# Wider reads in the K, V and FFN weight loads of a decode block

## The chip, the cores and the metric

The kernel runs on one core of a Trainium2 chip. The metric is the device time of one execution in microseconds (us). It was measured three times; the median is what is compared. A profile of one further execution, taken by the hardware profiler, is read for the causes. In it PE is TensorE's matmuls, PEld its weight loads, DVE is VectorE, ACT ScalarE, POOL GpSimd, and SP (SPq) the queue of SyncE, which here only issues DMAs.

## The reference

One token for each of four batches goes through a layer norm; its output feeds attention over the last 4096 positions of a K/V cache and, in parallel, a gated feed-forward block. Both results are added to the input. All tensors are bfloat16.

```python
B, Sq, D = 4, 1, 512;  Hq, Hkv, Sk, Dh = 32, 8, 16384, 128;  F = 1792;  W = 4096
xn = layernorm(x)
q = (xn @ wq)                                     # 32 heads of 128
k, v = k_cache[:, :, Sk - W:, :], v_cache[:, :, Sk - W:, :]   # each of 8 kv heads serves 4 q heads
p = softmax(q k^T * Dh**-0.5)
A = (p v) @ wo
Bf = (silu(xn @ w_gate) * (xn @ w_up)) @ w_down
out = x + A + Bf
```

The K and V windows are 33.6 MB each, the weights about 14 MB together: the kernel reads 81.01 MB from HBM for four rows of output.

## The kernel before

The attention is cut into 16 steps (`ND`). Step d takes kv head d // 2 for two of the four batches (the first two where d is even, the last two where it is odd). Its K is 2 x 4096 rows of 128 values, 2 MB, and is loaded by one DMA as a tile of 128 partitions by 16 KB: a partition holds 64 (`NT`) consecutive positions of one batch. Function `kv_ap` (L167) gives the order of partitions: position group first, batch second, so partition 2q belongs to the first batch and 2q + 1 to the second. V is loaded by the same pattern. K and V each have two buffers (`KB`, `VB`), taken in turn.

For each step TensorE transposes K in 64 pieces of 128 x 128 (L386), VectorE copies the transposes from PSUM to SBUF (L300), and TensorE computes scores for the 8 heads of both batches against every partition. Since a partition belongs to one batch, the scores of the other batch's heads are pushed to minus 1e30 by a small matmul (`mask`, L377) that multiplies `mkr`, a 2 x 128 table of which partition is whose, by `mkc`. GpSimd builds `mkr` at the start (L190, L205). Then come the row maximum (L305), the shift (L405), the exponential (L271), the denominators and the product with V (`pv`, L409). The first half of a step's V product runs while the next step's scores run.

SyncE issues all the large loads on one queue, in this order: W_q (`WQ`); K of steps 0 and 1; W_gate and W_up (`WG`, `WU`); V of step 0; then K of step d and V of step d - 1 for d = 2 to 15; W_down (`WD`); V of step 15 in two halves of each partition's row (`load_v_half`, L232); and W_o (`WO`) in five pieces cut by `WO_CUTS`. K of step d waits until step d - 2's transposes are finished (`s_tr`), V of step d until the product of the step before is finished (`s_pv`, the counter starts with one). WG, WU and WD hold rows of 14 KB in each of 128 partitions, `WQ` rows of 32 KB. The two halves of the last V have semaphores of their own (`d_v[1]` and `d_vz`), so that TensorE can begin with the first half (L461) and waits for the second at L462.

After the 16 steps TensorE multiplies W_gate and W_up (L452), the last V, W_down, and then the 32 rows of W_o (`out_rows`, L171), each piece behind its semaphore. `spin` (L424) issues matmuls whose results nobody reads. Two copies and one 4 KB DMA write the output.

Of the kernel before, what the change touches and what calls it, by code (L numbers as in the profile page):

```python
# [2 lines left out]

# [2 lines left out]
ALU = mybir.AluOpType  # L6
# [4 lines left out]
def bass_parallel_sum__sliding_block_cached__swiglu_ffn__decode_kernel(  # L11
# [13 lines left out]
    _, HKV, Sk, Dh = A_k_cache.shape  # L25
    HQ = A_wq.shape[1] // Dh
    F = B_w_gate.shape[1]
    W = min(4096, max(256, Sk // 4))
# [6 lines left out]
    ND = B * HKV // 2  # L35
    C = 2 * REP
    NT = 2 * W // 128
    HT = NT // 2
    NG = 4
    KVN = NT * Dh  # L40
    HKN = HT * Dh
    SN = NT * C
# [11 lines left out]
    WG = sb("wg_sb", [128, NC, F], BF16)  # L54
    WU = sb("wu_sb", [128, NC, F], BF16)
    WD = sb("wd_sb", [128, NF, D], BF16)
    WO = sb("wo_sb", [128, NO, D], BF16)
    KB = sb("kbuf", [128, 2 * KVN], BF16)
    VB = sb("vbuf", [128, 2 * KVN], BF16)
# [6 lines left out]
    mkr = sb("mkr", [2, 128], BF16)  # L66
# [49 lines left out]
    d_wg = sem("d_wg")  # L116
    d_wu = sem("d_wu")
    d_wd = sem("d_wd")
# [3 lines left out]
    d_k = [sem("d_k%d" % s) for s in range(2)]  # L122
    d_v = [sem("d_v%d" % s) for s in range(2)]
    d_vz = sem("d_vz")
# [36 lines left out]
    wg_ap = B_w_gate.rearrange("(p c) n -> p c n", c=NC)  # L161
    wu_ap = B_w_up.rearrange("(p c) n -> p c n", c=NC)
    wd_ap = B_w_down.rearrange("(p t) n -> p t n", t=NF)
    wo_ap = A_wo.rearrange("(p c) n -> p c n", c=NO)
    ds = bass.ds

    def kv_ap(cache, d):  # L167
        b0 = d % 2 * 2
        return cache[b0:b0 + 2, d // 2, Sk - W:, :].rearrange("b (q t) d -> q b (t d)", t=NT)

    def out_rows(eng, c0, c1):  # L171
        for c in range(c0, c1):
# [7 lines left out]
    with nc.Block() as block:  # L180

        @block.gpsimd
        def _(eng):
            eng.memset(ident[:], 0.0)
            eng.memset(I4[:], 0.0)
            eng.memset(I8[:], 0.0)
            eng.memset(I4w[:], 0.0)
            eng.memset(rep[:], 0.0)
            eng.memset(ones[:], 1.0)
            eng.memset(mkr[:], -BIG)  # L190
            eng.memset(mkc[:], 1.0)
            eng.drain()
            eng.affine_select(I4[:], I4[:], pattern=[[-1, B]], compare_op=ALU.not_equal,
                              fill=1.0, base=0, channel_multiplier=1)
            eng.affine_select(ident[:], ident[:], pattern=[[-1, 128]], compare_op=ALU.not_equal,
                              fill=1.0, base=0, channel_multiplier=1)
            eng.affine_select(I8[:], I8[:], pattern=[[-1, C]], compare_op=ALU.not_equal,
                              fill=1.0, base=0, channel_multiplier=1)
            eng.affine_select(I4w[:], I4w[:], pattern=[[-1, 64]], compare_op=ALU.not_equal,
                              fill=1.0, base=0, channel_multiplier=1)  # L200

            eng.affine_select(rep[:], rep[:], pattern=[[1, REP], [-1, 128]], compare_op=ALU.not_equal,
                              fill=1.0, base=0, channel_multiplier=REP)

            eng.affine_select(mkr[:], mkr[:].rearrange("j (q b) -> j q b", b=2),  # L205
                              pattern=[[0, 64], [-1, 2]], compare_op=ALU.not_equal,
                              fill=0.0, base=0, channel_multiplier=1)
            eng.affine_select(mkc[:], mkc[:].rearrange("j (b h) -> j b h", b=2),
                              pattern=[[-1, 2], [0, REP]], compare_op=ALU.is_equal,
                              fill=0.0, base=0, channel_multiplier=1)  # L210
            eng.memset(XnT[:].bitcast(FP32), 0.0)
            eng.memset(QZ[:].bitcast(FP32), 0.0)
            eng.drain()
            eng.engine_nop().then_inc(s_const, 1)
            eng.memset(P[:], 1.0)
            eng.memset(VB[:, HKN:].bitcast(FP32), 0.0)  # L216
            eng.drain()
            eng.engine_nop().then_inc(s_const, 1)
            eng.engine_nop().then_inc(d_v[1], 16)

        @block.sync
        def _(eng):
            def load_k(d):
                if d >= 2:
                    eng.wait_ge(s_tr, 2 * NG * (d - 1))
                eng.dma_start(KB[:, d % 2 * KVN:(d % 2 + 1) * KVN], kv_ap(A_k_cache, d)).then_inc(d_k[d % 2], 16)

            def load_v(d):
                eng.wait_ge(s_pv, d + 1)
                eng.dma_start(VB[:, d % 2 * KVN:(d % 2 + 1) * KVN], kv_ap(A_v_cache, d)).then_inc(d_v[d % 2], 16)  # L230

            def load_v_half(d, h, done):  # L232
                a = d % 2 * KVN + h * HKN
                eng.dma_start(VB[:, a:a + HKN], kv_ap(A_v_cache, d)[:, :, h * HKN:(h + 1) * HKN]).then_inc(done, 16)

            def load_wo(n):
                a, b = WO_CUTS[n], WO_CUTS[n + 1]
                eng.dma_start(WO[:, a:b, :], wo_ap[:, a:b, :]).then_inc(d_wo[n], 16)

            eng.dma_start(WQ[:], wq_ap).then_inc(d_wq, 16)  # L240

            eng.wait_ge(s_xc, 1)
            load_k(0)
            load_k(1)
            eng.dma_start(WG[:], wg_ap).then_inc(d_wg, 16)
            eng.dma_start(WU[:], wu_ap).then_inc(d_wu, 16)
            load_v(0)
            for d in range(2, ND):
                load_k(d)
                load_v(d - 1)  # L250
            eng.dma_start(WD[:], wd_ap).then_inc(d_wd, 16)
            eng.wait_ge(s_pv, ND)
            load_v_half(ND - 1, 0, d_v[1])
            load_v_half(ND - 1, 1, d_vz)
            for n in range(len(d_wo)):
                load_wo(n)
# [19 lines left out]
        def _(eng):  # L276
# [17 lines left out]
            last.then_inc(s_qz, 1)  # L294
            eng.engine_nop().then_inc(s_ev, NG)

# [59 lines left out]
        def _(eng):  # L356
# [52 lines left out]
            def pv(bank, s, n):  # L409
                p = bank * PS  # L410
                if s == 0:
                    eng.wait_ge(d_v[bank], n[0])
                    eng.wait_ge(s_p, n[1])
                    eng.wait_ge(s_nrm, n[1])
                    for j in range(SN // 128):
                        mm(den_ps, ones[:], P[:, p + 128 * j:p + 128 * (j + 1)], start=(j == 0))
                for t in range(HT):
                    a = bank * KVN + s * HKN + 128 * t
                    o = p + C * (s * HT + t)
                    last = mm(O_wide, VB[:, a:a + 128], P[:, o:o + WIDE], start=(s == 0 and t == 0))  # L420
                if s == 1:
                    last.then_inc(s_pv, 1)
# [11 lines left out]
            with eng.Fori(0, ND // 2) as r:  # L434
                for b in range(2):
                    n = 2 * r + (b + 1)
                    ev = 4 * NG * r + 2 * NG * b
                    q = lambda w, b=b: QF[:, ds(r * (2 * WIDE) + b * WIDE, w)]
# [19 lines left out]
                last.then_inc(done, 1)  # L458
            for n in range(2):
                mm(ps_acc[64 * n:64 * n + 64, 0:256], I4w[:], X[:, 256 * n:256 * n + 256], start=True)  # L460
            pv(1, 0, (8 * ND + 16, ND + 1))  # L461
            eng.wait_ge(d_vz, 16)  # L462
            pv(1, 1, None)
            eng.wait_ge(s_guT, 1)
            eng.wait_ge(d_wd, 16)
# [58 lines left out]
```

## Time and profile before

| What | Value |
|---|---|
| Time, median of 3 | 195.99 us (195.85, 195.99, 196.53) |
| The profiled execution's own time | 195.84 us |
| Its span, first to last instruction | 194.6 us |
| Granted TensorE clock | 1.000 |
| PE busy, DVE busy | 161.6 us, 114.7 us |
| Read from HBM | 81.01 MB, 416 GB/s over the span |

The span is what the trace shows; 1.24 us of the profiled execution's time lie outside it. The DMA lines of a page count packets. SP's queue is called q1 there: it carried 6048 packets. 42 DMAs of 128 rows are 5376 rows, and each DMA ends with one 4-byte write on each of 16 DMA engines, which makes 672 more: 6048. So at present each row of a destination partition is one packet. The share of a queue is the sum of its packets' recorded durations over 16 engines' time; as the records of neighbouring packets overlap a little, it can pass 100%.

### The profile page before, as it was taken

How to read it: one execution, taken by the hardware profiler on the slowest of the kernel's cores; microseconds unless marked ns; L12 is line 12 of the kernel's file. 1: busy time of each engine (PE TensorE's matmuls, PEld its weight loads, DVE VectorE, ACT ScalarE, POOL GpSimd, SP SyncE). 2: the span in 40 equal slices, each digit the busy share in tenths (PEclk: the TensorE clock that was granted, in tenths of full speed). 3: DMA queues.
4: the chain of work that ended last, by engine and by line, in shares of the span. 5: the costliest groups of instructions: out<-in, count | busy, mean ns of one | idle time of the engine just before them, and what ended most of it. 6: DMA issues, size and time to landing. Idle time of an engine off the chain costs nothing. (4 is left out here: it accounts for less than half of the span.)

```text
span 194.6 us, 7758 instructions
## 1 busy us (share of the span) xinstructions
PE 161.6 (83%) x3466; PEld 138.9 (71%) x3466; DVE 114.7 (59%) x250; ACT 17.0 (9%) x27; POOL 10.3 (5%) x23
## 2 busy tenths in 40 slices
PE   0127997549898989898989898989898989898995
PEld 0113895548888878787878787878787878787752
DVE  1004775527676767676767676767676767675620
ACT  5700101001010101010101010101010101010100
POOL 8930000000000000000000000000000000000000
DMA  6999999999999999999999999999999999999992
GB/s 216 431 428 431 440 428 419 433 424 431 431 431 431 431 431 431 431 431 431 431 431 431 434 431 431 431 431 431 431 431 431 431 431 431 431 429 421 436 412 111
DMA packets 6070, 81.10 MB, mean 417 GB/s; under 512 B 680, under 2 KB 816, under 8 KB 1072
## 3 DMA queue, kind: packets, MB, share of 16 engines
q1 hardware_dynamic: 6048, 81.01, 97.7%
q8 instruction: 5, 0.08, 0.1%
q10 hardware_dynamic: 16, 0.01, 0.0%
q14 instruction: 1, 0.01, 0.0%
HBM read 81.01 MB, written 0.00 MB: 416 GB/s over the span
## 5 line engine op out<-in xcount | busy, mean ns | idle before, releaser
L300 DVE COPY kT<-ps_kt 128x1024 bf16<-128x1024 bf16 x128 | 79.4, 683 | 27.7 <-PE ps_kt L386 27.7
L386 PE MATMUL ps_kt<-ident,kbuf 128*128 128x128 bf16 x1024 | 62.8, 219 | 12.9 <-DMA kbuf<-in_A_k_cache_dram 11.9
L386 PEld LDWEIGHTS ps_kt<-ident,kbuf 128*128 128x128 bf16 x1024 | 57.3, 98 | 18.2 <-issue 18.2
L358 PE MATMUL ps_o<-p,vbuf 128*128 128x64 bf16 x1120 | 38.4, 193 | 0.0
L358 PEld LDWEIGHTS ps_s<-qz,kT 128*128 128x128 bf16 x1024 | 31.4, 98 | 6.6 <-issue 3.6
L358 PEld LDWEIGHTS ps_o<-p,vbuf 128*128 128x128 bf16 x1120 | 35.2, 98 | 1.1
L358 PE MATMUL ps_s<-qz,kT 128*128 x1024 | 34.7, 192 | 1.2
L271 ACT ACTIVATE p<-ps_s 128x512 bf16<-128x512 f32 x17 | 10.1, 597 | 162.1 <-PE ps_s L358 162.1
L305 DVE TENSOR_REDUCE rm<-ps_s 128x8 bf16<-128x512 f32 x17 | 11.7, 691 | 21.2 <-PE ps_s L358 21.2
L358 PE MATMUL ps_o<-p,ones 128*128 128x128 bf16 (+1 forms) x69 | 6.9, 220 | 3.3 <-DMA vbuf<-in_A_v_cache_dram 2.0
L358 PE MATMUL ps_kt<-wq_sb,xnT 128*32 128x512 bf16 x32 | 3.6, 624 | 5.3 <-DMA wq_sb<-in_A_wq_dram 5.3
L358 PEld LDWEIGHTS ps_o<-p,ones 128*128 128x128 bf16 x69 | 4.5, 98 | 4.5 <-DMA vbuf<-in_A_v_cache_dram 2.2
L363 PE MATMUL ps_acc<-i,xn 4*128 4x4 f32 x4 | 0.6, 254 | 7.4 <-ACT xn L268 7.4
L358 PE MATMUL ps_s<-mkc,mkr 2*128 2x512 bf16 x17 | 6.5, 385 | 0.0
L358 PE MATMUL ps_s<-dg,ones 8*128 8x512 bf16 x17 | 6.5, 385 | 0.0
L288 DVE STREAM_TRANSPOSE kT<-ps_kt 128x512 f32<-128x512 f32 x2 | 1.4, 716 | 8.0 <-PE ps_kt L358 8.0
L358 PEld LDWEIGHTS ps_kt<-wq_sb,xnT 128*32 128x32 bf16 x32 | 1.2, 137 | 6.8 <-issue 6.8
L363 PEld LDWEIGHTS ps_acc<-i,xn 4*128 4x128 f32 x4 | 0.6, 207 | 7.4 <-issue 7.4
L316 DVE TENSOR_REDUCE den<-ps_o 128x8 f32<-128x128 f32 x18 | 4.9, 274 | 1.0 <-PE ps_o L358 1.0
L216 POOL MEMSET vbuf<- 128x6144 f32 x1 | 5.2, 5222 | 0.0
L310 DVE TENSOR_REDUCE m<-ps_acc 8x1 f32<-8x128 f32 x17 | 4.6, 268 | 0.3 <-PE ps_acc L358 0.3
L320 DVE TENSOR_TENSOR oT<-ps_o,den 128x8 f32 (+1 forms) x18 | 3.0, 166 | 2.9 <-issue 2.7
(68 smaller groups left out, 50.3 us busy)
## 6 DMA issues: line engine op xcount, KB each, us to landing
kbuf<-in_A_k_cache_dram SPq DMA_DIRECT2D x16, 2048.0 KB, 12.6
vbuf<-in_A_v_cache_dram SPq DMA_DIRECT2D x15, 2048.0 KB, 11.3
wq_sb<-in_A_wq_dram SPq DMA_DIRECT2D x1, 4096.0 KB, 12.4
vbuf<-in_A_v_cache_dram SPq DMA_DIRECT2D x2, 1024.0 KB, 9.2
wo_sb<-in_A_wo_dram SPq DMA_DIRECT2D x1, 2048.0 KB, 14.4
wg_sb<-in_B_w_gate_dram SPq DMA_DIRECT2D x1, 1792.0 KB, 23.8
wu_sb<-in_B_w_up_dram SPq DMA_DIRECT2D x1, 1792.0 KB, 27.3
wd_sb<-in_B_w_down_dram SPq DMA_DIRECT2D x1, 1792.0 KB, 15.0
```

The lines of the kernel that those rows point to most:

```text
L216: eng.memset(VB[:, HKN:].bitcast(FP32), 0.0)
L271: eng.activation(P[:, d % 2 * PS:d % 2 * PS + SN], ps_S[d % 2][:], ACT.Exp, scale=SCALE).then_inc(s_p, 1)
L288: eng.transpose(qT[:, 512 * n:512 * n + 512], ps_kt[n][:])
L300: eng.tensor_copy(KT[:, u * HKN + 1024 * g:u * HKN + 1024 * (g + 1)], kt_ps[g].rearrange("p a b -> p (a b)")).then_inc(s_ev, 1)
L305: eng.tensor_reduce(RM[:], ps_S[bank][:].rearrange("p (t c) -> p c t", c=C), AX.X, ALU.max).then_inc(s_rm, 1)
L310: eng.tensor_reduce(m8[:], mt_ps, AX.X, ALU.max)
L316: eng.tensor_reduce(den[:], den_ps.rearrange("p (t c) -> p c t", c=C), AX.X, ALU.add)
L320: eng.tensor_tensor(OT[:, 2 * b:2 * b + 2, ds(r * REP, REP)], O_ps.rearrange("p (j h) -> p j h", j=2), den[:].rearrange("p (j h) -> p j h" ...
L358: return eng.matmul(o, l, r, start=start, stop=stop, skip_group_check=True)
L363: last = eng.transpose(xT_ps[:, c * B:(c + 1) * B], xn[:].rearrange("b (p c) -> b c p", c=NC)[:, c, :], I4[:])
L386: last = eng.transpose(kt_ps[g][:, k, :], KB[:, a:a + 128], ident[:])
```

## The change

A load's DMA carries two access patterns, one for what is read and one for what is written. Before, both were cut at the same places: one partition's row. Now a new helper, `load`, builds the DMA as before and then exchanges the pattern of the read for one with longer contiguous pieces. The written pattern stays one row for each partition.

* K and V, 31 of the 33 loads: the read pieces are 32 KB, two partitions' rows (`FOLD` = 2).
* W_gate, W_up, W_down: the read pieces are 56 KB, four partitions' rows (`fold_rows`).
* For that, two partitions that are neighbours must hold neighbouring positions of one batch. `kv_ap` now groups 128 positions, so partitions 4q and 4q + 1 belong to the first batch and 4q + 2 and 4q + 3 to the second. The table `mkr` follows: its pattern has one more dimension.
* The halves of the last V can't be read in one piece with the partition beside them. Each half is now two DMAs of 64 partitions, one for the even and one for the odd ones, with 8 KB read and written at a time as before. The semaphores `d_v[1]` and `d_vz` are waited for at values that are 16 higher.
* The copied instruction carries `ant_dge_precooked=False`, a flag on how the issuing queue takes the DMA in.

```diff
+    FOLD = 2
-    def kv_ap(cache, d):
+    def kv_ap(cache, d, fold):
         b0 = d % 2 * 2
-        return cache[b0:b0 + 2, d // 2, Sk - W:, :].rearrange("b (q t) d -> q b (t d)", t=NT)
+        return cache[b0:b0 + 2, d // 2, Sk - W:, :].rearrange("b (q t) d -> q b (t d)", t=fold * NT)
+
+    def load(eng, to, rows, pieces):
+        with nc.discard():
+            by_row = eng.dma_start(to, rows).ins
+        whole = replace(by_row.ins[0], ap=pieces.ap, bass_ap=pieces)
+        return eng.add_instruction(replace(by_row, name=nc.get_next_instruction_name(), ins=[whole],
+                                           ant_dge_precooked=False))
+
+    def fold_rows(w):
+        return w.rearrange("(p c) n -> p (c n)", p=32)
+
+    def load_kv(eng, buf, cache, d):
+        return load(eng, buf[:, d % 2 * KVN:(d % 2 + 1) * KVN], kv_ap(cache, d, 1), kv_ap(cache, d, FOLD))
...
-            eng.affine_select(mkr[:], mkr[:].rearrange("j (q b) -> j q b", b=2),
-                              pattern=[[0, 64], [-1, 2]], compare_op=ALU.not_equal,
+            eng.affine_select(mkr[:], mkr[:].rearrange("j (q b i) -> j q b i", b=2, i=FOLD),
+                              pattern=[[0, 64 // FOLD], [-1, 2], [0, FOLD]], compare_op=ALU.not_equal,
                               fill=0.0, base=0, channel_multiplier=1)
...
-                eng.dma_start(KB[:, d % 2 * KVN:(d % 2 + 1) * KVN], kv_ap(A_k_cache, d)).then_inc(d_k[d % 2], 16)
+                load_kv(eng, KB, A_k_cache, d).then_inc(d_k[d % 2], 16)
...
-                eng.dma_start(VB[:, d % 2 * KVN:(d % 2 + 1) * KVN], kv_ap(A_v_cache, d)).then_inc(d_v[d % 2], 16)
+                load_kv(eng, VB, A_v_cache, d).then_inc(d_v[d % 2], 16)
 
             def load_v_half(d, h, done):
                 a = d % 2 * KVN + h * HKN
-                eng.dma_start(VB[:, a:a + HKN], kv_ap(A_v_cache, d)[:, :, h * HKN:(h + 1) * HKN]).then_inc(done, 16)
+                for i in range(FOLD):
+                    b = i * KVN + h * HKN
+                    eng.dma_start(VB[i:128:FOLD, a:a + HKN], kv_ap(A_v_cache, d, FOLD)[:, :, b:b + HKN]).then_inc(done, 16)
...
-            eng.dma_start(WG[:], wg_ap).then_inc(d_wg, 16)
-            eng.dma_start(WU[:], wu_ap).then_inc(d_wu, 16)
+            load(eng, WG[:], wg_ap, fold_rows(B_w_gate)).then_inc(d_wg, 16)
+            load(eng, WU[:], wu_ap, fold_rows(B_w_up)).then_inc(d_wu, 16)
...
-            eng.dma_start(WD[:], wd_ap).then_inc(d_wd, 16)
+            load(eng, WD[:], wd_ap, fold_rows(B_w_down)).then_inc(d_wd, 16)
...
-            pv(1, 0, (8 * ND + 16, ND + 1))
-            eng.wait_ge(d_vz, 16)
+            pv(1, 0, (8 * ND + 16 * FOLD, ND + 1))
+            eng.wait_ge(d_vz, 16 * FOLD)
```

The one place where instructions are added is the end of SyncE's queue. Before, it read so from the last full V load on (partitions x elements of what is written, and the semaphore that an issue waits for):

```order
L230 DMA vbuf<-in_A_v_cache_dram 128x1x8192 [waits s_pv]
L251 DMA wd_sb<-in_B_w_down_dram 128x7168
L234 DMA vbuf<-in_A_v_cache_dram 128x1x4096 [waits s_pv]
L234 DMA vbuf<-in_A_v_cache_dram 128x1x4096
L238 DMA wo_sb<-in_A_wo_dram 128x8192
L238 DMA wo_sb<-in_A_wo_dram 128x5120
L238 DMA wo_sb<-in_A_wo_dram 128x1536
```

Behind the two V halves stand the pieces of W_o, of which three are shown. With the change the same stretch reads (L178 is the helper `load`):

```order
L178 DMA vbuf<-in_A_v_cache_dram 128x1x8192 [waits s_pv]
L178 DMA wd_sb<-in_B_w_down_dram 128x7168
L255 DMA vbuf<-in_A_v_cache_dram 64x1x4096 [waits s_pv]
L255 DMA vbuf<-in_A_v_cache_dram 64x1x4096 x3
L259 DMA wo_sb<-in_A_wo_dram 128x8192
L259 DMA wo_sb<-in_A_wo_dram 128x5120
L259 DMA wo_sb<-in_A_wo_dram 128x1536
```

Two issues became four, and the pieces of W_o stand two issues further back. On every other engine the same instructions stand in the same order.

More of the change, by code (lines that the diff above doesn't have):

```diff
@@ L1 @@
+from copy import replace
 import concourse.bass as bass
```

## The prediction

> **What bounds the kernel now.** I read the page's slices first, then the waits, then the end of the timeline. The head of the page, with the two DMA rows of its slices and the queue's line:
>
> ```profile
> span 194.6 us, 7758 instructions
> PE 161.6 (83%) x3466; PEld 138.9 (71%) x3466; DVE 114.7 (59%) x250; ACT 17.0 (9%) x27; POOL 10.3 (5%) x23
> ...
> DMA  6999999999999999999999999999999999999992
> GB/s 216 431 428 431 440 428 419 433 424 431 431 431 431 431 431 431 431 431 431 431 431 431 434 431 431 431 431 431 431 431 431 431 431 431 431 429 421 436 412 111
> ...
> q1 hardware_dynamic: 6048, 81.01, 97.7%
> ```
>
> The DMA engines are full from the first slice to the last, at a rate that stands at 431 GB/s through the whole loop. No compute engine is full. SP's queue fills 97.7% of 194.6 us, 190 us; what is left is about what passes before the first packet and after the last. So the time is a short head, 81 MB at the engines' pace, and a short tail.
>
> The list of waits says the same from TensorE's side, and a row of the timeline shows one such wait, the last of them:
>
> ```profile
> PE ps_kt L386 <- DMA kbuf<-in_A_k_cache_dram: 11.9, 14, 2.7
> ```
>
> ```profile
> 168.77 1.96 PE L386 MATMUL ps_kt<-ident,kbuf 128*128 128x128 bf16 x32 [0.70 <-DMA kbuf<-in_A_k_cache_dram]
> ```
>
> TensorE waits for K in most steps, 11.9 us over 14 waits, and typically 0.7 us in a pair of steps that lasts 9.7 us. Compute has that much room before it would bind: the DMA pace could rise by some 7% first. The end of the timeline:
>
> ```profile
> 189.56 0.82 PE L358 MATMUL ps_s<-kbuf,ident 128*128 128x512 bf16 x3
> 190.67 1.29 PEld L176 LDWEIGHTS ps_acc<-wo_sb,oP 128*4 128x4 bf16 x26 [0.79 <-DMA wo_sb<-in_A_wo_dram]
> ...
> 192.22 0.09 PEld L176 LDWEIGHTS ps_acc<-wo_sb,oP 128*4 128x4 bf16 x4 [0.25 <-DMA wo_sb<-in_A_wo_dram]
> 192.56 0.08 PEld L176 LDWEIGHTS ps_acc<-wo_sb,oP 128*4 128x4 bf16 x2 [0.25 <-DMA wo_sb<-in_A_wo_dram]
> ...
> 192.88 0.41 DVE L490 CAST y_sb<-ps_acc 4x256 bf16<-4x256 f32 x1 [5.46 <-PE ps_acc L176]
> ```
>
> The last three pieces of W_o are each waited for, so the DMA sets the end as well. Whatever takes a nanosecond from every engine's stream takes it from the time.
>
> **The price of a packet.** The change moves the same bytes; it alters how many pieces they are read in. So I need what a piece costs beside its bytes. Two stretches of the queue with very different pieces give it: the steady loop, 60 to 150 us, and the end, 188.7 to 190.5 us, where W_o's short rows run.
>
> ```profile
> DMA packets 2661, 38.80 MB, mean 431 GB/s; under 512 B 293, under 2 KB 293, under 8 KB 293
> ...
> q1 hardware_dynamic: 2661, 38.80, 100.7%
> ```
>
> ```profile
> DMA packets 285, 0.71 MB, mean 396 GB/s; under 512 B 31, under 2 KB 81, under 8 KB 268
> ...
> q1 hardware_dynamic: 285, 0.71, 99.3%
> ```
>
> Let a packet be recorded with b ns plus a ns for each byte. Share times 16 engines times the stretch is the sum of the records: 1.007 x 1,440,000 = 1,450,080 ns in the first, 0.993 x 28,800 = 28,598 ns in the second. So 38.80 million a + 2661 b = 1,450,080 and 0.71 million a + 285 b = 28,598, which gives b = 8.7 ns and 16 KB = 602.6 ns. The records overlap, however: 0.7% of 1,440,000 ns is 10,080 ns, 3.8 ns for each packet. A packet's fixed price in real time is thus 8.7 - 3.8 = 4.9 ns (4.2 to 5.7 for the rounding of 0.71 MB). It checks: 16 engines at 16 KB in 602.6 ns would be 435 GB/s, and 4.9 ns more a row, with the completion writes, brings that to the 431 of the rows.
>
> In the kernel before, a packet is one read and one write of the same size, so the trace cannot say whose price the 4.9 ns are. That is the open question here.
>
> **The change part by part.**
>
> *Reads of K and V.* 31 loads of 128 rows are 8 rows for each of 16 engines: 248 reads an engine become 124. Of the weights, 3 x 8 = 24 become 6. Saved: 124 + 18 = 142 reads an engine. If the price goes with the read: 142 x 4.9 = 0.70 us (0.60 to 0.81). If it goes with the write, which stays one row: nothing. The record's own 8.7 ns are the largest price that a row allows, 1.24 us. Below nothing: a write row that begins in the middle of a read may cost something that no row shows; up to the same 4.9 ns it eats the gain, and beyond it the change loses. Between the ends I take the whole 0.70 us. The nearest row is W_q's, whose pieces are already 32 KB; from 3 to 9 us only they run:
>
> ```profile
> DMA packets 79, 2.59 MB, mean 431 GB/s; under 512 B 0, under 2 KB 0, under 8 KB 0
> ...
> q1 hardware_dynamic: 79, 2.59, 100.4%
> ```
>
> 100.4% of 96,000 ns over 79 is 1220 ns a packet, against 2 x (602.6 + 8.7) = 1222.6 for two of K's: a 32 KB piece shows no price of its own for its length, so far as that stretch (79 whole packets in 6 us) can tell. It is read and written in 32 KB, so the write's part stays unknown.
>
> The Trainium skill speaks to this in "DMA: Bandwidth & Descriptors", section "Why small descriptors are slow (HBM only)": about 3 cycles a packet on the bus between the reading and the writing half, and merging worth it only at 256 bytes or less. That speaks against a change at 16 KB; with the page's 850 MHz the 3 cycles are 3.5 ns, and 142 of them an estimated 0.50 us, against 0.70 by the rows. The rows agree that there is a fixed price, and no run here yet shows which half bears it.
>
> *The last V.* The same 16 pieces of 8 KB an engine, in four DMAs for two: two more completion writes an engine, at the same 4.9 ns: +0.01 us. Two more issues stand ahead of W_o:
>
> ```profile
> L234 SPq DMA_DIRECT2D vbuf<-in_A_v_cache_dram x2: 542/574/607, 171.9 to 172.5; - x2
> ```
>
> ```profile
> wo_sb<-in_A_wo_dram SPq DMA_DIRECT2D x1, 2048.0 KB, 14.4
> ```
>
> W_o's issues come 2 x 0.6 = 1.2 us later. W_o's first piece lands 14.4 us after its issue and needs 4.9 us at 431 GB/s, so it sat some 9.5 us behind other transfers; that covers the 1.2 us. Without cover it would cost them whole.
>
> *The mask table.* One more dimension in one GpSimd instruction of 0.70 us:
>
> ```profile
> 3.53 0.70 POOL L205 TENSOR_SCALAR_AFFINE_SELECT mkr<-mkr 2x128 bf16<-2x128 bf16 x1
> ...
> 6.08 5.22 POOL L216 MEMSET vbuf<- 128x6144 f32 x1
> ...
> 18.20 0.27 PE L358 MATMUL ps_o<-p,ones 128*128 128x256 bf16 x1 [1.32 <-DVE qz L291]
> ```
>
> GpSimd ends at 11.3 us, and TensorE needs its work at 18.2 us, after a wait for something else. Even a doubled instruction is covered by 6.9 us. The mask matmuls keep shape and number.
>
> *Issue of the wide loads.* K's issues take 0.53 to 0.62 us and land 12.6 us later, for a transfer of 4.9 us:
>
> ```profile
> L226 SPq DMA_DIRECT2D kbuf<-in_A_k_cache_dram x16: 534/535/616, 3.3 to 156.1; - x16
> ...
> DMA to landing us min/median/max: 12.5/12.6/19.0
> ```
>
> So 7.7 us of other transfers stand ahead of each. If the exchanged pattern or its flag made an issue even three times as long, this queue would hide it: nothing.
>
> *What moves with it.* TensorE's last wait for K is at 168.77 us; by then all but the last V (4) and W_down (6) have given their savings, 132 of 142. From there TensorE runs without a DMA wait until W_o, so its chain comes 132 x 4.9 = 0.65 us earlier while W_o lands 0.69 us earlier. The 0.79 us before the second piece of W_o hardly changes, and nothing new becomes late.
>
> **Sum.** 0.70 - 0.01 = 0.69 us. The profiled execution took 195.84 us (194.6 in the span, 1.24 around it), which makes 195.15. It lies 0.15 us under the median of the runs, 195.99; on the median the forecast is 195.3 us.
>
> **The rivals.**
>
> 1. *The write keeps the price.* Each partition's row is still a write of its own, and if that half sets the 4.9 ns, the engines go on at 431 GB/s: 196.0 us (a third of the price saved: 195.76). For it: the number of writes does not change, and each engine's stream must pass its writing half. Against it: only that reads and writes were always paired, so nothing favours the one.
>
> 2. *The halves of the last V use fewer paths into the SBUF* (slower). Now they run so, from 175.8 to 180.6 us:
>
> ```profile
> DMA packets 275, 2.06 MB, mean 429 GB/s; under 512 B 31, under 2 KB 31, under 8 KB 31
> ```
>
> With 64 partitions in one DMA, should half of the rate be lost, the 2.10 MB take 4.9 us more, and W_o stands behind them: 195.3 + 4.9 = 200.2 us. It decides from a loss of 0.7 us, 13% of that stretch's rate. The Trainium skill, in "SBUF — State Buffer", section "Door 1: The DMA port swizzle (why `[64,N]` ≈ `[32,N]`)", measures partitions 0 to 63 at 196 GB/s against 328 for all 128, and puts it down to ports; by the same section's formula every second partition touches all 16 ports. No run here shows a 64-partition load. Against the rival: the even partitions spread as wide as all of them do.
>
> 3. *Every change of row within a read stalls.* 142 switches an engine at 8.7 ns, the record's whole price, without any saving: 195.99 + 1.24 = 197.2 us. For it: no trace here has a read that spans two writes. Against it: 16 KB behind each switch is long for an engine to prepare the next.
>
> 4. *More than the sum*: the record's price is all real, 195.99 - 1.24 = 194.75 us. The overlap speaks against it.
>
> **How the numbers follow.** A change of 0.3% of 195.99, 0.59 us, is about what a measurement of this kernel can tell from none; the three runs themselves span 0.68 us. The forecast gets 0.50, own range 195.0 to 195.6; rival 1 0.33; rivals 2 and 3 0.05 each; rival 4 0.07. The forecast's 0.69 us lie just past the limit: two thirds of its chance count as faster, the rest as the same. Faster: 0.33 + 0.07 = 0.40. Slower: rivals 2 and 3, 0.10. The same: 0.17 + 0.33 = 0.50. The range takes in rival 1 with its scatter and most of the price's bounds, 194.9 to 196.2; outside stay rivals 2 and 3 and the far end of 4.
>
> **What would show it.** In the loop, half a price less a row is 2.45 ns of some 608: the slices should read 433 instead of 431; 431 means rival 1, less rival 3. The last V's stretch should stay near 429; 215 to 370 means rival 2. K's wait of 0.7 us in a pair of steps should stay, since TensorE is paced by K's landing. The three waits for W_o at the end should stay at about 0.8, 0.25 and 0.25 us, all 0.7 us earlier; if the first goes and the time gains less than the landing, the chain from the last K binds. I am wrong if the rate rises and the end doesn't follow, or if the time moves by more than 1.2 us either way.

## The result, and the profile after

| | Median | Lowest to highest | Runs |
|---|---|---|---|
| Before | 196.11 us | 195.75 to 197.13 | 18 |
| After | 195.51 us | 195.31 to 197.16 | 18 |

The ratio of after to before is 0.9965, with a 95% interval of 0.995 to 0.9981. The kernel became faster by 0.35%, 0.69 us by the ratio and 0.60 us by the medians. The profiled execution took 195.45 us, 0.39 us less than the one of before.

The head of the page of after, its clock row, its DMA rows by slices, and the two lines on packets:

```profile
span 194.2 us, 7760 instructions
...
PEclk9999999988999999999999999999999999999999
...
DMA  6999998999999999999999999999999999998992
GB/s 224 425 439 432 564 393 346 425 430 439 412 432 432 432 432 432 432 432 432 432 432 432 432 432 439 432 452 432 432 432 432 432 439 432 432 472 353 437 407 107
...
DMA packets 3830, 81.10 MB, mean 418 GB/s; under 512 B 712, under 2 KB 848, under 8 KB 1104
...
q1 hardware_dynamic: 3808, 81.01, 97.4%
```

The same 81.01 MB come in 3808 packets, where there were 6048. The difference is 142 reads on each of 16 engines, 2272, less the 32 completion writes of the two added DMAs: the profile now counts a packet for each read, whatever number of writes it feeds. The slices look alike in both kernels because they come in steps: 64 pieces of 32 KB in a slice of 4.855 us are 432 GB/s, 65 are 439. A change of 0.35% is read from a long window, and even there a rate moves by 1 GB/s with the packets that happen to lie at its edges. The DMA view of 70 to 165 us, in which only K and V run, of the kernel before:

```profile
DMA packets 2812, 41.01 MB, mean 432 GB/s; under 512 B 309, under 2 KB 309, under 8 KB 309
...
q1 hardware_dynamic: 2812, 41.01, 100.8%
```

And of the kernel after:

```profile
DMA packets 1565, 41.13 MB, mean 433 GB/s; under 512 B 310, under 2 KB 310, under 8 KB 310
...
q1 hardware_dynamic: 1565, 41.13, 100.4%
```

In the prediction's window, 60 to 150 us, the rate does not show the change: 431 GB/s in both kernels. After:

```profile
DMA packets 1478, 38.83 MB, mean 431 GB/s; under 512 B 293, under 2 KB 293, under 8 KB 293
```

The packets' own records are finer than the rate. Of the sum of the records (share times 16 engines times 95 us, 1,520,000 ns), the 4-byte completion writes take 8.7 ns each. That leaves 611.1 ns for each of 2503 pieces of 16 KB before, and 1213.9 ns for each of 1255 pieces of 32 KB after: 8.2 ns less than two pieces of 16 KB. One overlap of two records, 3.8 ns, goes with it, so a read that is saved gives 4.4 ns of real time. The rounding of the shares to 0.1% leaves about 1 ns of doubt on that. 124 reads of K and V make 124 x 4.4 = 0.55 us of an engine's stream, and with the weights' 18 it is about 0.6 us.

TensorE still waits for K. First the group of waits, then the last such wait in the timeline:

```profile
PE ps_kt L407 <- DMA kbuf<-in_A_k_cache_dram: 10.3, 12, 2.9
```

```profile
168.26 1.96 PE L407 MATMUL ps_kt<-ident,kbuf 128*128 128x128 bf16 x32 [0.67 <-DMA kbuf<-in_A_k_cache_dram]
...
187.36 1.91 PE L194 MATMUL ps_acc<-wo_sb,oP 128*4 128x256 bf16 x32 [0.19 <-DMA wo_sb<-in_A_wo_dram]
189.21 0.82 PE L379 MATMUL ps_s<-kbuf,ident 128*128 128x512 bf16 x3
190.33 2.11 PE L194 MATMUL ps_acc<-wo_sb,oP 128*4 128x256 bf16 x32 [0.30 <-PEq L198]
192.16 0.08 PEld L194 LDWEIGHTS ps_acc<-wo_sb,oP 128*4 128x4 bf16 x2 [0.23 <-DMA wo_sb<-in_A_wo_dram]
192.48 0.41 DVE L511 CAST y_sb<-ps_acc 4x256 bf16<-4x256 f32 x1 [5.58 <-PE ps_acc L194]
```

The wait for K is 0.67 us (0.70 before) and lies 0.51 us earlier. The last wait for W_o and the copy behind it lie 0.40 us earlier. So in this one execution not all of the 0.6 us reached the end. TensorE also waits 0.19 us for W_o's first piece here, which it did not before.

The waits for K give the pace of the loop in real time, without the rounding of a share. Before, one of them ends here, ten pairs of loads ahead of the one at 168.77 us that the prediction shows:

```profile
71.52 1.96 PE L386 MATMUL ps_kt<-ident,kbuf 128*128 128x128 bf16 x32 [0.69 <-DMA kbuf<-in_A_k_cache_dram]
```

After, one ends here, nine pairs ahead of the one at 168.26 us:

```profile
81.02 1.96 PE L407 MATMUL ps_kt<-ident,kbuf 128*128 128x128 bf16 x32 [0.68 <-DMA kbuf<-in_A_k_cache_dram]
```

A pair takes 9.725 us before and 9.693 after (9.726 and 9.694 in the second profiles below). The 0.032 us belong to 8 saved reads: 4.0 ns for each, within the doubt on the 4.4 above. All 142 saved reads make 0.57 us by it.

The places that the prediction priced at nothing, first the issues of SP's queue by line, with the landing of W_o:

```profile
L178 SPq DMA_DIRECT2D kbuf<-in_A_k_cache_dram x16: 534/535/611, 3.0 to 155.6; - x16
...
L255 SPq DMA_DIRECT2D vbuf<-in_A_v_cache_dram x4: 534/599/600, 171.4 to 173.3; - x4
...
L259 SPq DMA_DIRECT2D wo_sb<-in_A_wo_dram x5: 431/432/589, 173.9 to 176.0; - x5
...
DMA to landing us min/median/max: 13.3/16.1/16.3
```

Then the mask table's instruction, and the DMA view of the last V's stretch, 176.2 to 180 us:

```profile
3.56 0.87 POOL L223 TENSOR_SCALAR_AFFINE_SELECT mkr<-mkr 2x128 bf16<-2x128 bf16 x1
```

```profile
DMA packets 247, 1.61 MB, mean 425 GB/s; under 512 B 50, under 2 KB 50, under 8 KB 50
...
q1 hardware_dynamic: 247, 1.61, 100.9%
```

An issue of a wide load lasts 0.53 us as before. The mask costs 0.17 us more and is covered. The four DMAs of 64 partitions run at 425 GB/s, against 429 before, with twice as many completion writes among their pieces. From the landing of W_down to that of W_o's first piece, on the mean of the 16 engines, 9.84 us pass, 9.85 before: nothing is lost there. W_o is issued from 173.9 us, and its first piece lands at least 13.3 us later.

### The profile page after: what moved, and what is told of

It is laid out like the page before. It is cut to its first block, busy times and chain, and to the rows that moved or that the text cites. A ratio compares the mean times of both kernels' runs of the same rounds, so it can differ in the third digit from the quotient of the medians.

```text
span 194.2 us, 7760 instructions
## 1 busy us (share of the span) xinstructions
PE 164.6 (85%) x3466; PEld 141.6 (73%) x3466; DVE 115.3 (59%) x250; ACT 17.0 (9%) x27; POOL 10.5 (5%) x23
## 3 DMA queue, kind: packets, MB, share of 16 engines
q1 hardware_dynamic: 3808, 81.01, 97.4%
HBM read 81.01 MB, written 0.00 MB: 417 GB/s over the span
## 5 line engine op out<-in xcount | busy, mean ns | idle before, releaser
L407 PE MATMUL ps_kt<-ident,kbuf 128*128 128x128 bf16 x1024 | 65.6, 224 | 11.2 <-DMA kbuf<-in_A_k_cache_dram 10.3
L407 PEld LDWEIGHTS ps_kt<-ident,kbuf 128*128 128x128 bf16 x1024 | 60.0, 101 | 16.5 <-issue 16.5
L379 PE MATMUL ps_o<-p,vbuf 128*128 128x64 bf16 x1120 | 38.4, 193 | 0.0
L379 PEld LDWEIGHTS ps_s<-qz,kT 128*128 128x128 bf16 x1024 | 31.4, 98 | 6.8 <-issue 3.6
L379 PEld LDWEIGHTS ps_o<-p,vbuf 128*128 128x128 bf16 x1120 | 35.2, 98 | 1.1
L379 PE MATMUL ps_s<-qz,kT 128*128 x1024 | 34.8, 192 | 1.2
L379 PE MATMUL ps_kt<-wq_sb,xnT 128*32 128x512 bf16 x32 | 3.6, 629 | 5.5 <-DMA wq_sb<-in_A_wq_dram 5.5
L379 PE MATMUL ps_o<-p,ones 128*128 128x128 bf16 (+1 forms) x69 | 7.0, 222 | 1.6 <-DVE qz L312 1.3
L379 PE MATMUL ps_s<-mkc,mkr 2*128 2x512 bf16 x17 | 6.8, 398 | 0.0
L379 PE MATMUL ps_s<-dg,ones 8*128 8x512 bf16 x17 | 6.5, 385 | 0.0
L379 PEld LDWEIGHTS ps_o<-p,ones 128*128 128x128 bf16 x69 | 4.5, 98 | 2.7 <-issue 2.2
L379 PEld LDWEIGHTS ps_kt<-wq_sb,xnT 128*32 128x32 bf16 x32 | 1.2, 137 | 7.1 <-issue 7.1
## 6 DMA issues: line engine op xcount, KB each, us to landing
wo_sb<-in_A_wo_dram SPq DMA_DIRECT2D x1, 2048.0 KB, 13.3
wd_sb<-in_B_w_down_dram SPq DMA_DIRECT2D x1, 1792.0 KB, 14.9
```

What stands on the lines that cost most here:

```text
L379: return eng.matmul(o, l, r, start=start, stop=stop, skip_group_check=True)
L407: last = eng.transpose(kt_ps[g][:, k, :], KB[:, a:a + 128], ident[:])
```

## The experiments

The theory: each read packet costs an engine some 4.9 ns beside its bytes, and the write rows cost nothing that shows. Against it stood: the pieces' writes set the price (rival 1), the saving came from elsewhere (the exchanged order of positions, the split of the last V), or the end of the kernel, not the stream, decides. Every experiment keeps the computation and the bytes.

### The two kernels again

The changed kernel, unchanged:

> The changed kernel once more, unaltered, for a second profile. Theory: the loop saves 4.7 to 4.9 ns for each read that falls away, and in the first profile of the changed kernel some of that was lost near 50 to 60 us, where the granted clock stood at 0.83 for a while just before and the DMA engines had gaps. In a profile without such a stretch the last piece of W_o should land about 0.65 us earlier than in the kernel before; with one, 0.4 to 0.5 us. On the median 0.60 to 0.69 us faster. Rival (the loss is in the tail, by the four DMAs of the last V): the gain at the last piece of W_o stays at 0.4 us in any profile.

It took 195.46 us (195.33 to 197.52, 12 runs), ratio 0.9975 (0.995 to 1.0001, an interval that just reaches no change). And the kernel before, unchanged:

> The kernel before once more, unaltered, for a second profile to set beside the two of the changed kernel. If the smaller gain at the end of the changed kernel's profiles (0.4 us at the last piece of W_o, where its loads' engines gain 0.6 us on average) comes from which engine happens to be last, this profile's last piece lands some 0.1 to 0.3 us off the first one's 192.5 us while the loop's K landings keep their 4.862 us; if it is the change's own tail, it lands within 0.05 us.

It took 195.99 us (195.87 to 196.50, 8 runs), ratio 0.9991 (0.9976 to 1.0007). The changed kernel's medians are thus 195.46 and 195.51, those of before, here and beside the other kernels, 195.99 to 196.13. The second profile of each shows how far one profile may be trusted at the end; first the changed kernel's last wait for W_o, then that of before:

```profile
192.09 0.08 PEld L194 LDWEIGHTS ps_acc<-wo_sb,oP 128*4 128x4 bf16 x2 [0.24 <-DMA wo_sb<-in_A_wo_dram]
```

```profile
192.66 0.08 PEld L176 LDWEIGHTS ps_acc<-wo_sb,oP 128*4 128x4 bf16 x2 [0.24 <-DMA wo_sb<-in_A_wo_dram]
```

Before it stood at 192.56 and 192.66, after at 192.16 and 192.09: 0.40 to 0.57 us earlier. The trace also holds when each of the 16 engines finished its share of that piece. On their mean it landed at 191.42 and 191.45 us before, at 191.00 and 190.89 after: 0.42 us earlier in the first profiles and 0.56 in the second. So the second profile, as expected, shows nearly the whole gain of the stream, and the loss in the first is not the tail's, nor that of one late engine.

### 64 partitions in a DMA, with 16 KB pieces

The kernel before, with each of the 31 K and V loads cut into two DMAs, one for the even partitions and one for the odd ones; the waits on their semaphores count 32 for 16:

```diff
+    def load_kv(eng, buf, cache, d, done):
+        for i in range(2):
+            rows = cache[d % 2 * 2 + i, d // 2, Sk - W:, :].rearrange("(q t) d -> q (t d)", t=NT)
+            eng.dma_start(buf[i:128:2, d % 2 * KVN:(d % 2 + 1) * KVN], rows).then_inc(done, 16)
...
```

> The kernel before, with each of the 31 whole K and V loads cut into two DMAs of 64 partitions (one for the even partitions, one for the odd), 16 KB read and 16 KB written at a time as before. Theory (an engine's stream pays a fixed price for each packet and bytes at a constant rate, whichever partitions it writes): 31 more completion writes an engine at 4.9 ns, so +0.15 us, about 0.1% over the kernel before. Rival (64 partitions reach fewer paths into the SBUF): the loop's 65 MB at half of 431 GB/s, some 150 us more. Even a loss of 5% in rate would show as 7 us.

It took 196.62 us (10 runs, before 196.10), ratio 1.0023 (1.0005 to 1.0041). The DMA view of the same 95 us:

```profile
DMA packets 3123, 40.93 MB, mean 431 GB/s; under 512 B 625, under 2 KB 625, under 8 KB 625
...
q1 hardware_dynamic: 3123, 40.93, 100.8%
```

All of K and V now goes through DMAs of every second partition, and the rate is 431 GB/s: no path is lost, and rival 2 falls. The kernel takes 0.52 us more where 0.15 were expected, but 0.42 of them lie outside the span: its runs take 1.63 to 1.70 us more than their spans, those of the kernel before 1.20 to 1.30. Why is open; the changed kernel, with two added DMAs, has 1.20 to 1.32. In the loop a pair of loads takes 9.736 us, by two waits that lie ten pairs apart:

```profile
71.82 1.96 PE L392 MATMUL ps_kt<-ident,kbuf 128*128 128x128 bf16 x32 [0.71 <-DMA kbuf<-in_A_k_cache_dram]
...
169.18 1.96 PE L392 MATMUL ps_kt<-ident,kbuf 128*128 128x128 bf16 x32 [0.72 <-DMA kbuf<-in_A_k_cache_dram]
```

That is 0.011 us more than before for two more completion writes, 5.5 ns each, near the 4.9 by which they were counted.

### Both sides in 2 KB pieces

The same two DMAs, with both patterns cut into eight:

```diff
...
+            a, b = rows.rearrange("q (j t) -> q j t", j=8), to.rearrange("q (j t) -> q j t", j=8)
+            eng.add_instruction(replace(by_row, name=nc.get_next_instruction_name(), ant_dge_precooked=False,
+                                        ins=[replace(by_row.ins[0], ap=a.ap, bass_ap=a)],
+                                        outs=[replace(by_row.outs[0], ap=b.ap, bass_ap=b)])).then_inc(done, 16)
```

> As the kernel with two DMAs of 64 partitions, but K and V are read and written in pieces of 2 KB instead of 16 KB, both sides alike. 31 x 8 rows an engine become 8 pieces each: 1736 more packets an engine. At the 4.9 ns of the prediction (4.7 by the changed kernel's own packets) that is 8.2 to 8.5 us: about 204.5 us. Both theories, the read's price and the write's price, say the same here; it sets the scale.

It took 204.90 us (2 runs), ratio 1.0434 (1.0396 to 1.0473):

```profile
DMA packets 19549, 38.82 MB, mean 409 GB/s; under 512 B 593, under 2 KB 593, under 8 KB 19549
...
q1 hardware_dynamic: 19549, 38.82, 105.1%
```

Against the 64-partition kernel, 7 more pieces for each of 248 rows are 1736 an engine for 204.90 - 196.62 = 8.28 us: 4.8 ns a piece, when both its read and its write are counted (both kernels have the same 1.6 to 1.7 us outside the span). The prediction's price stands at 2 KB as at 16 KB. Which side bears it is still open here.

### Reads left alone, writes cut finer

The kernel before, with 16 KB reads and the written pattern alone cut: j is 8 here, and 2, 4 and 32 in three more.

```diff
+    def load_kv(eng, buf, cache, d):
+        to = buf[:, d % 2 * KVN:(d % 2 + 1) * KVN]
+        pieces = to.rearrange("p (j t) -> p j t", j=8)
+        with nc.discard():
+            by_row = eng.dma_start(to, kv_ap(cache, d)).ins
+        narrow = replace(by_row.outs[0], ap=pieces.ap, bass_ap=pieces)
+        return eng.add_instruction(replace(by_row, name=nc.get_next_instruction_name(), outs=[narrow],
+                                           ant_dge_precooked=False))
...
```

> The kernel before with K and V read in 16 KB as before, but written in pieces of 2 KB: 8 writes for one read, 1736 more writes an engine and not one read more. Theory (the fixed price belongs to the read, that is, to the packet): nothing, 196.0 us. Rival (the price belongs to the write): 8.2 to 8.5 us more, 204.5 us. Half and half: 200 us.

With 2 KB writes it took 199.65 us (4 runs), ratio 1.0165 (1.0136 to 1.0195): +3.55 us. That is neither the theory's nothing nor the 8.5 us of a price that sits on the writes; it lies near the half and half. The three others were to show whether every further write has a price of 2.1 ns, or only short ones have one.

> The same with writes of 8 KB: one more write for each of 248 reads an engine, as many as the changed kernel has, at half its length. If each write within a read costs 2.1 ns: 0.52 us more, 196.6 us, and the loop at 429 to 430 GB/s. If a write behind a long piece is free (in the changed kernel's trace a 32 KB read with two writes goes on as fast as W_q's with one): nothing, 196.1 us, 431 GB/s.

> The same with writes of 4 KB: three more writes for each of 248 reads an engine. At 2.1 ns each 1.6 us more, 197.7 us; if only short pieces pay and 4 KB is long enough, nothing; if it lies between, 0.3 to 1.2 us.

> The kernel before, K and V read in 16 KB and written in pieces of 512 bytes: 31 more writes for each of 248 reads an engine, 7688 in all. After the run with 2 KB pieces (3.6 us for 1736 more writes, 2.1 ns each): if every write that begins within a read has that price, whatever its size, 16 us more, 212 us. If the price is only met where pieces are short, and grows as they get shorter, more than that: with 4.9 ns each 38 us more, 234 us.

The view of the loop with 8 KB writes (2 in a read):

```profile
DMA packets 2804, 40.90 MB, mean 430 GB/s; under 512 B 308, under 2 KB 308, under 8 KB 308
...
q1 hardware_dynamic: 2804, 40.90, 100.7%
```

With 4 KB writes (4 in a read):

```profile
DMA packets 2793, 40.62 MB, mean 428 GB/s; under 512 B 314, under 2 KB 314, under 8 KB 314
...
q1 hardware_dynamic: 2793, 40.62, 100.6%
```

With 2 KB writes (8 in a read):

```profile
DMA packets 2745, 39.99 MB, mean 421 GB/s; under 512 B 304, under 2 KB 304, under 8 KB 304
...
q1 hardware_dynamic: 2745, 39.99, 100.7%
```

With 512 B writes (32 in a read):

```profile
DMA packets 2528, 36.70 MB, mean 386 GB/s; under 512 B 288, under 2 KB 288, under 8 KB 288
...
q1 hardware_dynamic: 2528, 36.70, 100.7%
```

Again only reads are counted, and small writes hide from the counts; they show in how long a read's record lasts. Worked out as for the two kernels above:

| Writes in a 16 KB read | Time (runs) | Ratio (95%) | Record of a read | More than with one write | max(4.7, 2.35 x writes) - 4.7 |
|---|---|---|---|---|---|
| 1 (before) | 196.08 (28) | 1 | 611.1 ns | 0 | 0 |
| 2 | 196.23 (10) | 1.0014 (0.9996 to 1.0033) | 612.2 ns | 1.1 ns | 0 |
| 4 | 197.36 (7) | 1.0059 (1.0039 to 1.0078) | 615.7 ns | 4.6 ns | 4.7 |
| 8 | 199.65 (4) | 1.0165 (1.0136 to 1.0195) | 626.0 ns | 14.9 ns | 14.1 |
| 32 | 217.05 (profiled) | none drawn | 682.2 ns | 71.1 ns | 70.5 |

From 8 to 32 writes a read gains 56.2 ns, 2.34 ns a write. With that price the first column of differences is met within 1.1 ns by a read price of 4.7 ns: two writes cost as much as one read and almost hide beside it, and from the third on each write shows. So a new theory, drawn from these four kernels and not tested by them: an engine pays for reads and for writes side by side, the writes at a lower price, and the larger sum shows. Against 2.1 ns for every further write stand the rows with 2 and 32 writes, where it would make 2.1 and 65 ns for the 1.1 and 71.1 measured; against a price that grows as writes get shorter stands the last row, where a write of 512 B costs about as much as one of 2 KB. The times agree: 248 reads an engine x 4.6 ns are 1.14 us of the 1.28 measured with 4 writes, and 248 x 14.9 are 3.70 of the 3.55 with 8. With 32 writes, 248 x 71.1 are 17.6 of 21.0 us; its other run, at a granted clock of 0.918 for 0.953, took 230.44 us. What adds the rest there is open. In that kernel's trace an issue of K or V also lasts about 5 us (0.60 with 2 KB writes), nearly the 5.4 us of a load, so that row alone would not tell an engine's price from a limit of the issue.

By the waits for K a pair of loads takes 9.740 us with 2 writes, 9.816 with 4 and 9.969 with 8, over 9.725 with one: 0.9, 5.7 and 15.2 ns for each read. Between the last two a write costs 2.4 ns, so the price does not rest on the row with 32. And the second write is not quite free; about 1 ns of it shows.

### Wide reads, with their writes cut in two

If the theory of two prices holds, the change's gain should vanish when each 32 KB read of K and V feeds four writes of 8 KB in place of two of 16 KB. From the changed kernel:

```diff
     def load_kv(eng, buf, cache, d):
-        return load(eng, buf[:, d % 2 * KVN:(d % 2 + 1) * KVN], kv_ap(cache, d, 1), kv_ap(cache, d, FOLD))
+        to = buf[:, d % 2 * KVN:(d % 2 + 1) * KVN]
+        halves, wide = to.rearrange("p (j t) -> p j t", j=2), kv_ap(cache, d, FOLD)
+        with nc.discard():
+            by_row = eng.dma_start(to, kv_ap(cache, d, 1)).ins
+        return eng.add_instruction(replace(by_row, name=nc.get_next_instruction_name(), ant_dge_precooked=False,
+                                           ins=[replace(by_row.ins[0], ap=wide.ap, bass_ap=wide)],
+                                           outs=[replace(by_row.outs[0], ap=halves.ap, bass_ap=halves)]))
```

> The changed kernel (32 KB reads of K and V) with their writes cut to 8 KB, four for a read. The runs so far fit two prices that an engine pays side by side, the larger of which counts: about 4.7 ns for each read and 2.35 ns for each write (a 16 KB read with 2, 4, 8 and 32 writes took 0.8, 5, 15 and 70 ns more than with one). By that 32 KB with one read and four writes cost 9.4 ns beside the bytes, as much as two reads did before: the change's gain on K and V is gone, 196.0 us, 431 GB/s in the loop. Theory of the prediction (the price is the read's alone): the gain stays, 195.5 us, 433 GB/s. Each write within a read at 2.1 ns whatever its neighbours: 4.7 + 3 x 2.1 = 11 ns, 196.2 us. If only short pieces pay, and 8 KB is long: 195.6 us.

It took 196.03 us (10 runs, before 196.13), ratio 0.999 (0.9964 to 1.0016):

```profile
DMA packets 1559, 40.93 MB, mean 431 GB/s; under 512 B 310, under 2 KB 310, under 8 KB 310
...
q1 hardware_dynamic: 1559, 40.93, 100.3%
```

A read's record lasts 1218.5 ns, 4.6 more than in the changed kernel; over 124 reads that is 0.57 us, and 196.03 - 195.51 is 0.52. The intervals of the two ratios overlap, but the fastest of these ten runs, 195.95 us, is slower than 25 of the changed kernel's 30. Two waits for K, ten pairs of loads apart:

```profile
71.76 1.96 PE L413 MATMUL ps_kt<-ident,kbuf 128*128 128x128 bf16 x32 [0.72 <-DMA kbuf<-in_A_k_cache_dram]
...
169.08 1.96 PE L413 MATMUL ps_kt<-ident,kbuf 128*128 128x128 bf16 x32 [0.71 <-DMA kbuf<-in_A_k_cache_dram]
```

A pair takes 9.732 us, 0.039 more than in the changed kernel and 0.007 more than before: the gain is gone in the loop. The order of positions, the mask, the split of the last V, the flag and the number of reads are the changed kernel's here. So the gain is the reads' price, and it is there only as long as the writes stay under it. The theory of two prices foretold this; the time cannot tell it from the 196.2 us of 2.1 ns for each write.

### The last V whole

The changed kernel, but the last V loaded as the others are, in one DMA with 32 KB reads; TensorE's first half then waits for the whole. This spares 12 reads and 3 completion writes on an engine, and 3 issues, and gives up the early half:

```diff
...
-            load_v_half(ND - 1, 0, d_v[1])
-            load_v_half(ND - 1, 1, d_vz)
+            load_kv(eng, VB, A_v_cache, ND - 1).then_inc(d_v[1], 16)
...
-            pv(1, 0, (8 * ND + 16 * FOLD, ND + 1))
-            eng.wait_ge(d_vz, 16 * FOLD)
+            pv(1, 0, (8 * ND + 16, ND + 1))
             pv(1, 1, None)
```

> The changed kernel with the last V loaded whole, by the same helper with 32 KB reads, instead of in four DMAs of half rows: an engine has 4 reads of 32 KB for 16 of 8 KB and one completion write for four. Theory: 12 x 4.7 + 3 x 5.9 = 75 ns off every engine's stream, so W_o lands 0.07 us earlier and the time follows, which a time cannot show but the trace may. TensorE begins the last V product when all of it has landed, some 0.2 us later than now; the 0.8 us for which it later waits for W_o cover that. Rival: TensorE's chain behind the last V has no such room, and the kernel gets 0.2 us or more slower.

It took 195.82 us (12 runs, before 196.08), ratio 0.9976 (0.9958 to 0.9994); the changed kernel, not measured beside it, stood at 195.46 and 195.51. The timeline of its TensorE:

```profile
182.07 0.40 PE L371 MATMUL ps_o<-p,ones 128*128 128x128 bf16 x4 [0.63 <-DMA vbuf<-in_A_v_cache_dram]
...
189.60 0.82 PE L371 MATMUL ps_s<-kbuf,ident 128*128 128x512 bf16 x3
190.72 1.91 PE L194 MATMUL ps_acc<-wo_sb,oP 128*4 128x256 bf16 x32 [0.30 <-PEq L198]
```

TensorE waits 0.63 us for the whole V, and from there its own chain sets the end: the block of W_o's later pieces starts 0.39 us later than in the changed kernel, and runs through its 32 matmuls in 1.91 us, without the stops that stretched it to 2.11. W_o's last piece landed at 192.00 us, against 192.12 and 192.05 in the two profiles of the changed kernel: the 0.07 us foreseen do not stand out from their scatter. The early half is worth more than the wide read. It also shows how little room lies between the stream and TensorE's chain: a delay of 0.6 us turns the end from the one to the other.

## Why the prediction was right

The forecast was a gain of 0.69 us, and the measured one is 0.69 by the ratio and 0.60 by the medians. That the first agrees to the last digit is luck: its interval reaches from 0.37 to 0.98 us, and the pace of the loop makes 0.57.

*The price of a packet* held for a piece that is read and written: 4.9 ns were drawn from two stretches of the trace of before, and 4.8 were measured with 2 KB pieces on both sides. As the gain of a saved read it was about a quarter too high: 4.4 in the records, 4.0 in the pace of the loop, and at TensorE's last wait for K, where the prediction had 132 x 4.9 = 0.65 us, 0.51 were measured, 3.9 ns a read. About 1 ns is what a second write beside a read still costs.

*That it is the reads' price* held for this change; of the reason only half did. The prediction left open which side bears it, and took a write to cost nothing or to take the whole place. It does neither: a write has a price of its own, 2.35 ns, half as large, paid beside the read's. Before, one write hid beside one read. A fold of two puts two writes beside one read, 4.7 ns against 4.7, and so takes nearly the whole gain. For the weights, folded by four, four writes would by the same account cost 9.4 ns a read, where four reads cost 18.8 before: 6 x 9.4 = 56 ns saved instead of 18 x 4.7 = 85, a difference too small to measure in the time. In the packets' records it shows for W_down alone: its reads of 56 KB lasted 2121 to 2122 ns, those of W_gate and W_up nearly all 2116, four reads of 14 KB before 2140. Why the two differ is open. By the account of two prices, a fold of four would also bring K and V no more than a fold of two; that was not run.

*The rivals.* The first, that the writes keep the price, falls with this, but was nearer than it looked: with 8 KB writes the same reads gain 0.10 us, within the scatter. The second, lost paths with 64 partitions, falls twice, at 425 GB/s in the stretch of the last V and at 431 over the whole loop of K and V. The Trainium skill, in "SBUF — State Buffer", section "Door 1: The DMA port swizzle (why `[64,N]` ≈ `[32,N]`)", has 64 neighbouring partitions slower and spreads every second one over all ports; the runs agree with the second half, and no run here loads neighbouring ones. The third, a stall at each change of row within a read, falls: the record of a 32 KB read with two rows is shorter than that of two reads. It comes back, in a sense, where a read feeds more than two writes. The fourth, that all 8.7 recorded ns are real, would have been 1.24 us.

The rule of the Trainium skill that spoke against the change, in "DMA: Bandwidth & Descriptors", section "Why small descriptors are slow (HBM only)", puts the fixed price at about 3 cycles and merging as worth it only at 256 bytes or less. Its estimate, 0.50 us, lies within the measured interval (0.37 to 0.98 us of 196.11); its limit does not hold here, since merging 16 KB pieces made this kernel faster by 0.35%.

*The places priced at nothing* were nothing: issues, mask, halves of V and the later issues of W_o, by the rows above.

*What moves with it* is where a step was off, without moving the sum. The prediction read the 0.79 us before the second piece of W_o as a wait for its landing, so that the DMA would set the end with room to spare. In the first profile of the changed kernel the filler matmuls of `spin` (L379) end at 190.03 us and the block starts 0.30 us later, put down to TensorE's own sequencer; with V loaded whole, where that piece had landed at 190.28 us, before the filler's end, the block again starts 0.30 us after the filler. In the second profiles of both kernels the same start, 0.30 and 0.34 us after the filler, is put down to W_o's landing. The piece landed at 190.63 us in the first profile of before and at 190.28 in that of after, 0.05 us ahead of the block in both. So chain and landing come almost together there, the 0.79 us of the weight loads were no measure of the DMA's lead, and only the short waits behind, of 0.23 us, are surely for the DMA.

In the profiled execution the gain at the end, 0.40 us, is smaller than the stream's 0.57. One difference of that execution is seen on TensorE: its granted clock fell to 0.83 between 40 and 50 us. The windows of after, whose columns are the stretch, its length, the busy times of PE, PEld, DVE, ACT and POOL, the granted clock, the mean DMA share and the GB/s:

```profile
40.00:50.00 10.00, 7.55 (x123) 6.83 (x124) 4.73 (x12) 0.60 (x1) 0.00 (x0) 0.83 1.05 445
```

The transposes and the V load that waits for what follows them, in the timeline of after:

```profile
42.45 3.42 PE L407 MATMUL ps_kt<-ident,kbuf 128*128 128x128 bf16 x32 [2.94 <-DMA kbuf<-in_A_k_cache_dram]
...
47.10 0.53 SPq L178 DMA_DIRECT2D vbuf<-in_A_v_cache_dram  x1
```

And of before, at the same place at the full clock:

```profile
42.46 1.96 PE L386 MATMUL ps_kt<-ident,kbuf 128*128 128x128 bf16 x32 [2.71 <-DMA kbuf<-in_A_k_cache_dram]
...
45.64 0.54 SPq L230 DMA_DIRECT2D vbuf<-in_A_v_cache_dram  x1
```

32 transposes took 3.42 us instead of 1.96, and the next V was issued 1.46 us later. The queue had loads ahead of it: the page's DMA row stays at 9 there. The landings, on the mean of the 16 engines, show a loss all the same: the same load lands at 50.59 us here and at 50.60 in the second profile of the changed kernel, the next at 55.56 and 55.45, and the last K at 167.11 and 166.93. So 0.1 to 0.2 us of the gain were lost between 50 and 70 us. That the clock did it is not shown; the second profile had its lower clock earlier, by the same view, and lost nothing of the kind:

```profile
26.00:40.00 14.00, 11.84 (x245) 10.45 (x240) 7.47 (x16) 0.60 (x1) 0.00 (x0) 0.88 1.00 429
```

Its last wait for W_o came 0.07 us before the first's.

Two things stay open: why a second write beside a read costs 1 ns where two prices side by side would let it hide, and what took 0.1 to 0.2 us from the stream of the first profile. The gain at the end, 0.40 to 0.57 us in the profiles and 0.60 to 0.69 in the medians and the ratio, agrees with the stream's 0.57 within this scatter.

No kernel tried was faster than the changed one.

## What to carry to other kernels

Where the DMA queue is full from end to end, the number of pieces an engine reads is a term of the time even at 16 KB: count the reads per engine, take the fixed price from two stretches of the trace with different piece sizes, less the overlap of the records, and multiply. Here that came out a quarter too high. Before folding rows into one read, count the writes too, because the larger of the two sums is what shows; here the second write to a read cost about 1 ns of the 4.9, and with four writes of 8 KB to a read of 32 KB the gain was gone. A load cut into parts so that its user can begin early is worth more than a few saved packets when the user's chain stands close behind the stream.

## What the runs showed of the hardware that was not expected

* An engine's prices for reads and for writes behave as if paid side by side, 4.7 and 2.35 ns, so that the larger sum shows; this fits the records of five kernels within 1.1 ns. The packet counts follow the reads alone: 32 writes of 512 B in a read left no small packet in the counts, and lengthened its record from 611.1 to 682.2 ns.
* Every second partition of a tile is as fast a target as all of them: 431 GB/s through the loop with 64 partitions in each DMA.
* A second DMA for each load slowed the loop by 5.5 ns a load, about the price of a packet; the kernel with 31 of them took 0.42 us more outside its span.
* The granted TensorE clock fell to 0.83 for some 10 us of a profiled execution, and a load that waits for TensorE was issued 1.46 us later.
